# Other places for the four quarters of the input's load, for its statistics and for products of ones, in an S4D and token-mixing layer

## The chip, the core and the metric

The kernel runs on one core of a Trainium2 chip. The engines of the core work side by side, each through its own instruction stream in order: TensorE (PE; its weight loads are listed as PEld), VectorE (DVE), ScalarE (ACT), GpSimd (POOL) and SyncE (SP), which here only issues DMAs. They wait for one another through semaphores. DMAs are issued from SP's queue, and a few from GpSimd, and are moved by sixteen DMA engines. The metric is the time of one execution on the device, in microseconds.

## The reference

The layer works on x, 2048 tokens of 448 channels. It has a conditioning vector, a diagonal state-space convolution along the tokens, and a two-layer perceptron across the tokens:

```python
mod = (_silu(c) @ w_mod).reshape(c.shape[0], 6, 1, -1)
sa, ca, ga, sb, cb, gb = (mod[:, 0], mod[:, 1], mod[:, 2], mod[:, 3], mod[:, 4], mod[:, 5])
h = _layernorm(x, axis=-1) * (1 + ca) + sa
x = x + ga * _A_ref(h, A_log_A_real, A_A_imag, A_C_real, A_C_imag, A_log_dt, A_D_skip)
h = _layernorm(x, axis=-1) * (1 + cb) + sb
x = x + gb * _B_ref(h, B_w1, B_b1, B_w2, B_b2)
```

`_A_ref` first makes a convolution kernel K for every channel, as a sum over 256 complex modes of `C * exp(A * dt * position)`, and then convolves by FFT:

```python
P = jnp.exp((A * dt[:, None])[:, :, None] * pos[None, None, :])
K = 2.0 * jnp.einsum("dn,dnl->dl", C, P).real
```

## The kernel before, in words

The program has two halves. The first makes K, takes the DFT of the normalized input and of K, multiplies them and transforms back; the second is the layer norm and the perceptron. Only the beginning of the first half is touched here.

**Steps.** K is made in 56 steps (`NHALF`), one for half a group of 16 channels. A step s has these parts: TensorE makes exponents (`st_exponents`) and phases (`st_phase`, two products of the table `tab` with parameter rows and two of a rounding constant with `ones`) in PSUM; ScalarE takes exponentials of the exponents (`st_exp`, tile mag) and six activations of the phases (absolute values and sines, L677 to L682); GpSimd makes m2 (`st_mag2`: a small w, then m2, L660 and L665) and the two halves of G (L684, L685); VectorE makes the four pieces of E (L686 to L690), with `between()` called in their middle; TensorE multiplies E with G into kg (`st_kgen`, L711) two steps later.

**Sets.** Exponential and sine come from different tables of ScalarE, so eight steps (`BATCH`) form a set: `window(s)` makes all eight exponentials and the first phase, and then the eight steps run with the sine table loaded. `window(0)` is a loop over e from 0 to 7; in its passes from e = 2 on it calls `st_mag2(e - 2)`, in the passes from e = 4 on `u_stats(e - 4)`, and in pass 3 four small copies of the skip weights on GpSimd.

**The input.** The tile xt holds x, 16 rows of 448 for each of 128 partitions. `x_load(r0, n, eng)` loads n of the 16 rows by four DMAs, one for each group of 32 partitions, from SP or from GpSimd. A quarter is four rows. `u_stats(r)` makes mean and variance of row r (L513 and L514); after all sixteen, in `window(8)`, ScalarE makes the reciprocal deviations, VectorE refines them (`u_scale`) and GpSimd scales a DFT table by them (`u_table`, L529), which the first products of the input's DFT (`u_rows`, L542) need. Before, the quarters are loaded like this: the first by GpSimd in `first_chain()`, between two of its splits; the second by SP as two pairs of rows, just ahead of the loop; the third and fourth by GpSimd at the ends of steps 1 and 2. Statistics of rows 0 to 3 are made in `window(0)`, those of rows 4 to 15 two at a time in `between()` of steps 2 to 7.

**Parameters.** `first_chain()` computes the parameter rows of the first 128 channels. SP loads them straight into lex (exponents) and lph (phases) for the first groups (L867), and stores them to DRAM (pars, L871) for the later ones. `more(n)` runs steps of the same chain for the next channels on VectorE.

**Modulation.** `wm_load(k, ...)` loads one of six 448 by 448 blocks of w_mod on SP (784 KB); `modulation(k, half)` multiplies it in two parts at the ends of steps: block 1 in steps 4 and 5, block 2 in steps 6 and 7.

**Order.** On TensorE, ScalarE, VectorE and GpSimd the order of the program text is the order of execution. On SP it is that too until step 8, from where a planner orders its DMAs. `late` lists what SP issues at the start of a step. `warm(n)` multiplies the constant `ones` into a part of a PSUM tile that holds nothing at the time; its result is not used.

Of the kernel before, what the change touches and what calls it, by code (L numbers as in the profile page):

```python
# [30 lines left out]
BATCH = 8  # L31
# [189 lines left out]
def tile_adaln_s4d_mixer(ctx, tc, i, out):  # L221
# [20 lines left out]
    with ExitStack() as es:  # L242
# [94 lines left out]
        def wm_slot(k):  # L337
# [3 lines left out]


        late = {
            4: lambda: wm_load(2, wm_slot(2)),
            7: lambda: wm_load(0, wm_slot(0)),
            6: lambda: [
                nc.sync.dma_start(wu, i["WU"]),
# [309 lines left out]
        def st_mag2(s):  # L657
            me = v32(mags[s][:, 0])
            w = wp.tile([P, GD], F32, tag="w", name="w")
            G.tensor_tensor(w[:, :, None], me[:, :, 31:32], me[:, :, 1:2], ALU.mult)  # L660
            if s in (3, 4, 5):
                m2 = v32(wm0.rearrange("p k d -> p (k d)")[:, -512 * (s - 2) :][:, 0:512])
            else:
                m2 = m2p[s >= 32 and s % BATCH > 2].tile([P, GD, 32], F32, tag="m2", name="m2")
            G.tensor_tensor(m2, me, w[:, :, None].to_broadcast([P, GD, 32]), ALU.mult)  # L665
            m2s[s] = m2
# [178 lines left out]
        def first_chain():  # L845
            cr, ci, a, aim = (raws[0][nm] for nm in ("A_C_real", "A_C_imag", "A_log_A_real", "A_A_imag"))
            xa, ya, s, t, u, ph, p64 = (
                qp.tile([P, N], F32, tag=nm, name=nm) for nm in ("xa", "ya", "s", "t", "u", "ph", "p64")
            )

            w = xp.tile([P, 2, D], F32, tag="yt", name="first", bufs=3)[:, 0, 0:N]

            def split(eng, src):

                hl = room.pop()
                eng.tensor_copy(hl[:, 0].bitcast(F32R), src)
                eng.tensor_tensor(hl[:, 1].bitcast(F32R), src, hl[:, 0], ALU.subtract)
                return hl

            room = wm0.rearrange("p k d -> p (k d)")[:, -12 * N :].rearrange("p (h j n) -> p h j n", h=6, j=2)  # L860
            room = [room[:, h] for h in range(6)]
            signs = room.pop()
            sr, si_ = signs[:, 0], signs[:, 1]

            def direct(hl, tile, r, g):

                nc.sync.dma_start(tile[g][r : r + 32].bitcast(F32), hl[16 * g : 16 * g + 16])  # L867

            def store(hl, *places):
                for k, v in places:  # L870
                    nc.sync.dma_start(pars[0][v, k], hl)  # L871

            S.activation(xa, cr, AF.Abs, scale=0.5)
            S.activation(ya, ci, AF.Abs, scale=0.5)
            S.activation(a, a, AF.Exp, bias=ldt0)
            S.activation(dt[:, 0:1], ldt0, AF.Exp)

            S.activation(one, one, AF.Ln)

            ts(sr, cr, 0.0, 0.5, ALU.is_ge, ALU.subtract)  # L880
            ts(si_, ci, 0.0, 0.5, ALU.is_ge, ALU.subtract)
            tt(s, xa, ya, ALU.add)
            tt(ya, ya, xa, ALU.subtract)
            ts(s, s, 2.0**-120, None, ALU.max)
            V.reciprocal(xa, s)
            ha = split(G, a)
            tt(ya, ya, xa, ALU.mult)
            ts(t, s, 2.0**-40, 2.0**80, ALU.is_lt, ALU.mult)
            stt(p64, t, 1.0, s, ALU.max, ALU.mult)
            for g in range(4):  # L890
                direct(ha, lex, 0, g)
                if g < 3:
                    direct(ha, lex, 64, g)
            par_load(1, par_names[0:2])
            x_load(0, 4, G)
            S.activation(u, ya, AF.Square)
            S.activation(u, u, AF.Ln, bias=1.0)
            S.activation(p64, p64, AF.Ln)
            S.activation(xa, ya, AF.Arctan)
            S.activation(xa, xa, AF.Copy, scale=4 * i2p, bias=-0.5)  # L900
            S.activation(dt[:, 1:4], ldt[:, 1:4], AF.Exp)
            S.activation(sc, cvec, AF.Exp, scale=-1.0)

            ts(dt4[:, 0:1], dt[:, 0:1], 1.0 / (4 * math.pi), None, ALU.mult)
            ts(ldt2[:, 0:1], ldt0, 1.5 * math.log(2.0), None, ALU.add)
            ts(ph, aim, dt4[:, 0:1], None, ALU.mult)
            ts(w, ph, MAGIC, MAGIC, ALU.add, ALU.subtract)
            stt(s, t, -80 * math.log(2.0) / 2.0**80, p64, ALU.mult, ALU.add)
            stt(s, u, 0.5, s, ALU.mult, ALU.add)
            ts(s, s, ldt2[:, 0:1], None, ALU.add)  # L910
            hs = split(V, s)
            for g in range(4):
                direct(hs, lex, 96, g)
                if g == 0:
                    direct(ha, lex, 64, 3)
            tt(ph, ph, w, ALU.subtract)
            hp = split(G, ph)
            direct(hp, lph, 0, 0)

            ts(w, ph, MAGIC7, MAGIC7, ALU.add, ALU.subtract)  # L920
            tt(p64, ph, w, ALU.subtract)

            tt(xa, xa, sr, ALU.mult)
            stt(xa, xa, 0.5, si_, ALU.add, ALU.mult)
            stt(xa, ph, 63.0, xa, ALU.mult, ALU.add)
            ts(u, xa, MAGIC, MAGIC, ALU.add, ALU.subtract)
            tt(xa, xa, u, ALU.subtract)
            store(ha, (0, 1), (1, 1))
            hl = split(G, p64)
            direct(hl, lph, 64, 0)  # L930
            hc = split(V, xa)
            direct(hc, lph, 96, 0)
            store(hs, (2, 1))
            store(hp, (0, 0))
            store(hl, (1, 0))
            store(hc, (2, 0))
# [2 lines left out]
        par_load(1, par_names[2:4])  # L939
        for g in (1, 2):  # L940
            load(g, False)
        x_load(4, 2)
        x_load(6, 2)
        wm_load(1, wm_slot(1))
        remainder()

        def chains():
# [43 lines left out]
        def window(s):  # L991
# [11 lines left out]
            for e in range(BATCH):  # L1003
                st_exp(s + e)

                if e + 1 < BATCH:
                    st_exponents(s + e + 1)
                else:
                    st_phase(s)
                mellow()  # L1010
                flush(dve)
                flush(act)
                if s == 8 and e == 0:
                    tt(mod[1], mod[1], mod[2], ALU.mult)
                if s < 32:
                    more(WPACE[s // 8][e])
                if s == 0 and e >= 4:
                    u_stats(e - 4)
                if s == 8 and e in (3, 4):
                    modulation(0, e - 3)  # L1020
                if s == 8 and e == 5:

                    G.tensor_tensor(mod[0], mod[0], mod[2], ALU.mult)
                if s and e < (2 if s <= 32 else 1):
                    st_kgen(s - (2 if s <= 32 else 1) + e)
                elif e == 5:
                    if s == 8:
                        yks[0] = y0.tile([P, 32, DC], F32, tag="yk", name="yk0")
                    st_s1(s > 16)

                for k, e0 in ((4, 1), (5, 3), (3, 6)) if s == 16 else ():
                    if e in (e0, e0 + 1):
                        modulation(k, e - e0)

                if s == 8:
                    warm(7)
                if s in (8, 16):
                    some(u_rows, rows, (2, 2, 2, 2, 2, 0, 1, 1)[e])
                elif s == 24 and e != 5:
                    some(u_cols, cols, 1)  # L1040

                if s >= 40 and e == 2:
                    piece(False, True)
                if s >= 40 and e == 4:
                    piece(pieces[0] < NP, True)
                if s == 0 and e > 1:
                    st_mag2(e - 2)
                elif s and (e < 2 or s >= 32):
                    st_mag2(s + e)
                if s == 0 and e == 3:  # L1050
                    for r in range(4):
                        dsk_copy(r)
            aside.clear()
            if s == 0:

                S.activation(one, one, AF.Sin)


# [4 lines left out]
        for s in range(tail):  # L1063
# [20 lines left out]

            def between():
                flush(dve)
                if 2 <= s < BATCH:
                    for r in range(2 * s, 2 * s + 2):
                        u_stats(r)
                if s < len(pace):  # L1090
                    more(pace[s])

# [4 lines left out]
            else:  # L1097
                if s < 32 and s % BATCH > 1:
                    st_kgen(s - 2)
                if s % BATCH < 2:  # L1100
                    warm(10)
                if (s + 1) % BATCH:
                    st_phase(s + 1)
                elif s + 1 < NHALF:
                    st_exponents(s + 1)
                if s == 7:
                    warm(10)

                if s > 32 and s % BATCH:
                    st_kgen(s - 1)  # L1110
# [3 lines left out]
                st_kgen(s - 1)  # L1114


            if s in (1, 2):
                x_load(4 + 4 * s, 4, G)
            free = s > 7 and not st_s1(s % BATCH == BATCH - 1)
            if s + 2 < 32 and (s + 2) % BATCH > 1 and s + 2 > 5:  # L1120
                st_mag2(s + 2)
# [276 lines left out]
```

## Time and profile before

| what | before |
|---|---|
| time, median of 3 runs | 698.44 us (696.92 to 700.45) |
| the profiled execution | 699.5 us, its span 697.7 us |
| TensorE busy | 646.5 us (93%) |
| VectorE busy | 424.1 us (61%) |
| ScalarE busy | 448.5 us (64%) |
| GpSimd busy | 274.7 us (39%) |
| DMA | 128.04 MB, mean 184 GB/s |

How to read it: times in the profile count from the start of the span. A row of the timeline has start, duration, engine, line of the program, operation, result and sources, and in brackets the engine's idle time ahead of it with what ended it. A row of the chain of waits has start, duration and who worked; "issue" is time in which an engine waited for nothing that the profile shows. A row of a stretch has its limits, its length, the busy time (and count) of TensorE, its weight loads, VectorE, ScalarE and GpSimd, then the granted TensorE clock as a share of the full one, the DMA engines' busy share and GB/s. A row of a DMA queue has packets, MB and the share of the sixteen engines' time.

### The profile page before, as it was taken

To read this page: it belongs to the slowest core of one execution; us is meant where nothing else is said; L and a number is where in the kernel's file an instruction comes from. 1 tells how busy PE (TensorE), PEld (TensorE's weight loads), DVE (VectorE), ACT (ScalarE), POOL (GpSimd) and SP (SyncE) were. 2 spreads that over 40 slices of the span, in tenths; PEclk is the share of its full clock that TensorE was granted. 3 is DMA by queue.
4 is the path that set the end of the run, shared out by engine and by line. 5 is a ranking of instruction groups with operands and counts; after the bars stand their busy time and mean duration, and the time that the engine had idled before them with its cause. 6 is when DMAs were issued, how large, how long until landed. Compare 5 with 4: busy or idle time off the path is not lost.

```text
span 697.7 us, 18532 instructions
## 1 busy us (share of the span) xinstructions
PE 646.5 (93%) x7314; PEld 486.1 (70%) x7314; DVE 424.1 (61%) x811; ACT 448.5 (64%) x841; POOL 274.7 (39%) x364
## 2 busy tenths in 40 slices
PE   0868999999988899999999989999999999999997
PEld 0444454455545676676789747778999999999996
DVE  7877889787575584857744368777622354444431
ACT  5787698899879899999766568877422332222220
POOL 6694669588588767777546200000000000000000
PEclk9998999999999999999999999999999999999999
DMA  7595647588785486554579899974683445555640
GB/s 183 178 194 143 214 163 241 212 234 268 213 266 165 126 170 170 145 157 120 142 235 301 257 278 244 236 177 135 174 247 108 146 132 159 159 158 165 169 129 28
DMA packets 101894, 128.04 MB, mean 184 GB/s; under 512 B 13547, under 2 KB 85231, under 8 KB 101807
## 3 DMA queue, kind: packets, MB, share of 16 engines
q1 hardware_dynamic: 100606, 123.31, 63.0%
q0 software_dynamic: 1200, 3.54, 2.4%
q8 instruction: 58, 0.95, 0.6%
q14 instruction: 30, 0.24, 0.1%
HBM read 91.46 MB, written 34.87 MB: 181 GB/s over the span
## 4 chain that ended last, share of the span: by engine, by line
PE 68%; ACT 10%; DMA 8%; DVE 6%; issue 4%; POOL 3%; SPq 1%; DVEq 0%; ACTq 0%; POOLq 0%
PE xe L621 7%; PE acc L1222 7%; PE o L1365 6%; PE o L1364 6%; PE o L1366 6%; PE acc L1223 6%; PE acc L1224 6%; PE kg L711 6%; DMA si<-in_SK_dram 3%; PE xg L621 3%; PE pu L542 2%; PE pu L574 2%; PE vv L820 2%; PE kx L804 2%; PE vv L821 2%
## 5 line engine op out<-in xcount | busy, mean ns | idle before, releaser
L206 ACT CAST whi<-w 128x896 fp32r<-128x896 f32 x64 | 59.8, 938 | 134.9 <-PE o L1365 84.6
L215 DVE TENSOR_TENSOR wlo<-w,whi 128x896 fp32r<-128x896 f32 x64 | 68.1, 1088 | 43.1 <-ACT whi L206 36.8
L684 POOL TENSOR_TENSOR G<-mag,gs 128x512 f32<-128x512 f32 x56 | 71.9, 1283 | 50.9 <-ACT gs L680 47.1
L1222 PE MATMUL acc<-h3h,whi 128*128 128x448 f32 x224 | 82.7, 369 | 0.8 <-ACT h3h L1273 0.8
L1223 PE MATMUL acc<-h3l,whi 128*128 128x448 f32 x224 | 81.5, 364 | 0.7 <-DVE h3l L1280 0.5
L1365 PE MATMUL o<-ul,whi 128*128 128x448 f32 x224 | 81.3, 363 | 0.0
L1364 PE MATMUL o<-uh,whi 128*128 128x448 f32 x224 | 81.2, 362 | 0.0
L1224 PE MATMUL acc<-h3h,wlo 128*128 128x448 f32 x224 | 80.7, 360 | 0.0
L1366 PE MATMUL o<-uh,wlo 128*128 128x448 f32 x224 | 80.6, 360 | 0.0
L711 PEld LDWEIGHTS kg<-E,G 128*32 128x32 f32 x3584 | 56.6, 114 | 32.3 <-issue 22.2
L711 PE MATMUL kg<-E,G 128*32 128x64 f32 x3584 | 66.4, 228 | 6.7 <-issue 6.1
L685 POOL TENSOR_TENSOR G<-mag,gs 128x512 f32<-128x512 f32 x56 | 71.8, 1282 | 0.0
L621 PE MATMUL xg<-tab,lph 64*128 64x512 f32 x112 | 62.3, 556 | 5.1 <-ACT gs L680 2.4
L621 PE MATMUL xe<-tab,lph 64*128 64x512 f32 x112 | 62.2, 555 | 1.1 <-ACT gs L681 0.9
L686 DVE TENSOR_TENSOR E<-m,xe 128x512 f32<-128x512 f32 x53 | 36.4, 687 | 41.3 <-ACT xe L679 24.3
L1368 DVE SCALAR_TENSOR_TENSOR y<-o,b,mod 128x448 f32<-128x448 f32 x16 | 10.9, 684 | 80.2 <-PE o L1366 80.2
L665 POOL TENSOR_TENSOR m<-mag,w 128x512 f32<-128x512 f32 x53 | 56.0, 1056 | 4.3 <-DMA u<-us_d 0.2
L1222 PEld LDWEIGHTS acc<-h3h,whi 128*128 128x128 f32 x224 | 42.0, 188 | 13.9 <-ACT h L1278 5.6
L812 DVE TENSOR_TENSOR z<-kx,u 128x448 f32<-128x448 f32 x48 | 28.4, 620 | 27.7 <-PE kx L804 27.7
L1223 PEld LDWEIGHTS acc<-h3l,whi 128*128 128x128 f32 x224 | 42.1, 188 | 3.3 <-DVE h3l L1280 0.8
L1364 PEld LDWEIGHTS o<-uh,whi 128*128 128x128 f32 x224 | 42.0, 188 | 3.4
L621 PE MATMUL xe<-tab,lex 64*128 64x512 f32 x56 | 28.9, 531 | 16.6 <-DMA lex<-wm 15.8
(233 smaller groups left out, 1512.1 us busy)
## 6 DMA issues: line engine op xcount, KB each, us to landing
w<-in_B_w_dram SPq DMA_DIRECT2D x64, 224.0 KB
w<-in_B_w_dram SPq DMA_DIRECT2D x32, 448.0 KB
u<-us_d SPq DMA_DIRECT2D x48, 224.0 KB
yu_d<-yt SPq DMA_DIRECT2D x16, 448.0 KB
yi<-yu_d SPq DMA_DIRECT2D x32, 224.0 KB
us_d<-uo SPq DMA_DIRECT2D x16, 448.0 KB
v_d<-vt SPq DMA_DIRECT2D x32, 224.0 KB
vt<-v_d SPq DMA_DIRECT2D x16, 448.0 KB
```

The lines of the kernel that those rows point to most:

```text
L206: self.nc.scalar.copy(hi, w)
L215: eng.tensor_tensor(lo, w, hi.bitcast(F32), ALU.subtract)
L621: T.matmul(out[k], lhs[r], rhs[r], start=start, stop=stop)
L684: G.tensor_tensor(Gt[:, 1], mg_, v32(sg), ALU.mult)
L685: G.tensor_tensor(Gt[:, 0], mg_, v32(cg_), ALU.mult)
L711: T.matmul(kg[32 * q : 32 * q + 32, m], Gt[:, c, d], E[:, c, d], start=h == 0 and c == 0 and m == 0, stop=h == 1 and c == 1, skip_group_ch ...
L1222: nc.tensor.matmul(acc[f], hi[:, fs], h3h[:, r], start=r == 0, stop=False)
L1223: nc.tensor.matmul(acc[f], hi[:, fs], h3l[:, r], start=False, stop=False)
L1224: nc.tensor.matmul(acc[f], lo[:, fs], h3h[:, r], start=False, stop=r == 15)
L1364: nc.tensor.matmul(o, hi[:, ks], uh[kh][:, k], start=kh == 0 and k == 0, stop=False)
L1365: nc.tensor.matmul(o, hi[:, ks], ul[kh][:, k], start=False, stop=False)
L1366: nc.tensor.matmul(o, lo[:, ks], uh[kh][:, k], start=False, stop=kh == 1 and k == 6)
```

## The change

- The first quarter is still loaded by GpSimd, but inside `window(0)`, between w and m2 of step 0.
- The second quarter is loaded by GpSimd, at the end of pass e = 4 of `window(0)`, and no longer by SP.
- The third quarter is loaded by SP behind `wm_load(1)`, ahead of the loop; the fourth by SP at the start of step 3, behind `wm_load(2)`, which moves from step 4 to step 3.
- Statistics: rows 0 to 3 as before; rows 4 and 5 at the end of `window(0)`; row 6 in step 0, row 7 in step 1, and two rows in each of steps 2 to 5.
- `warm(4)` is new in steps 2 to 7 (the products lie between `st_kgen` and `st_phase`); the `warm(10)` of step 7 becomes `warm(16)`.

```diff
         late = {
-            4: lambda: wm_load(2, wm_slot(2)),
+            3: lambda: [wm_load(2, wm_slot(2)), x_load(12, 4)],
...
             G.tensor_tensor(w[:, :, None], me[:, :, 31:32], me[:, :, 1:2], ALU.mult)
+            if s == 0:
+                x_load(0, 4, G)
...
             par_load(1, par_names[0:2])
-            x_load(0, 4, G)
...
-        x_load(4, 2)
-        x_load(6, 2)
         wm_load(1, wm_slot(1))
+        x_load(8, 4)
         remainder()
...
+                if s == 0 and e == 4:
+                    x_load(4, 4, G)
...
             if s == 0:
-
+                u_stats(4)
+                u_stats(5)
                 S.activation(one, one, AF.Sin)
...
                 flush(dve)
-                if 2 <= s < BATCH:
-                    for r in range(2 * s, 2 * s + 2):
-                        u_stats(r)
+                for r in ((6,), (7,), (8, 9), (10, 11), (12, 13), (14, 15))[s : s + 1]:
+                    for k in r:
+                        u_stats(k)
...
                 if s % BATCH < 2:
                     warm(10)
+                elif s < BATCH:
+                    warm(4)
...
                 if s == 7:
-                    warm(10)
+                    warm(16)
...
-            if s in (1, 2):
-                x_load(4 + 4 * s, 4, G)
```

## The prediction

> **What bounds the kernel now.** I read the page first (TensorE busy 93% of a 697.7 us span), then, because every edit lies in the first 70 us, the chain of waits of 26 to 75 us:
>
> ```profile
> 48.93 4.23 issue
> 53.16 0.43 PE kg L711 x6
> 53.60 0.72 PE xe L621
> ...
> 56.43 1.79 PE pm L498 x2
> ...
> 61.27 0.04 ACT ab L677
> ...
> 70.39 0.41 POOL wur L529
> ```
>
> The chain runs from engine to engine, so in this stage no engine alone sets the time. Its longest piece is no arithmetic: TensorE stands still for 4.23 us. What the chain feeds is the sine set: from 61.27, when ScalarE starts the last sines (step 7), a fixed sequence leads to the first scaled DFT table at 70.39. So **the moment the sines of step 7 can start is my measure**: what moves it moves all behind it.
>
> The timeline of VectorE says what holds step 7 back. It makes the E products (L686 to L690) of steps 0 to 7 and the statistics (L513) between them:
>
> ```profile
> 21.81 0.62 DVE L513 BATCH_NORM_STATS2 st<-xt 128x6 f32<-128x448 f32 x1
> ...
> 27.69 0.18 DVE L514 BATCH_NORM_AGGREGATE mv<-st 128x2 f32<-128x6 f32 x1
> 30.60 0.69 DVE L686 TENSOR_TENSOR E<-m,xe 128x512 f32<-128x512 f32 x1 [2.73 <-ACT xe L679]
> 31.21 0.68 DVE L687 SCALAR_TENSOR_TENSOR E<-mag,xe 128x512 f32<-128x512 f32 x1
> ...
> 32.55 1.38 DVE L415 SCALAR_TENSOR_TENSOR s<-t,s 128x256 f32<-128x256 f32 x1
> ...
> 51.52 0.63 DVE L513 BATCH_NORM_STATS2 st<-xt 128x6 f32<-128x448 f32 x1 [4.62 <-DMA xt<-in_A_u_dram]
> ...
> 52.28 0.59 DVE L513 BATCH_NORM_STATS2 st<-xt 128x6 f32<-128x448 f32 x1
> ...
> 57.43 0.68 DVE L690 TENSOR_TENSOR E<-wm,xg 128x512 f32<-128x512 f32 x1
> ```
>
> One row's statistics cost 0.76 us (52.28 minus 51.52), a piece of E 0.6 (31.21 minus 30.60), and two operations of the parameter chain in step 0 some 2.1 (31.8 to 33.9). VectorE idles 2.73 us before step 0 and 4.62 us in step 4, there for the third quarter of the input. GpSimd issues that quarter in step 1, and its own timeline shows the prices of issuing:
>
> ```profile
> 8.74 2.29 POOL L300 DMA_DIRECT2D xt<-in_A_u_dram  x4
> ...
> 15.27 0.78 POOL L857 TENSOR_TENSOR wm<-p,wm 128x256 fp32r<-128x256 f32 x1
> 17.27 0.27 POOL L660 TENSOR_TENSOR w<-mag 128x16 f32<-128x16 f32 x1 [1.23 <-ACT mag L644]
> 17.62 1.19 POOL L665 TENSOR_TENSOR m<-mag,w 128x512 f32<-128x512 f32 x1
> 21.23 0.30 POOL L660 TENSOR_TENSOR w<-mag 128x16 f32<-128x16 f32 x1 [2.42 <-ACT mag L644]
> ...
> 22.75 1.33 POOL L482 COPY dsk<-dskr 1x112 f32<-1x112 f32 x4
> ...
> 31.09 1.27 POOL L684 TENSOR_TENSOR G<-mag,gs 128x512 f32<-128x512 f32 x1 [1.42 <-ACT gs L680]
> ...
> 37.60 2.20 POOL L300 DMA_DIRECT2D xt<-in_A_u_dram  x4
> ...
> 42.26 2.20 POOL L300 DMA_DIRECT2D xt<-in_A_u_dram  x4
> ```
>
> How long such a quarter takes to arrive is in the view of the input tile, for these three groups of four DMAs (from issue to landing, shortest, median, longest):
>
> ```profile
> DMA to landing us min/median/max: 5.7/6.4/7.3
> DMA to landing us min/median/max: 8.5/10.3/12.1
> DMA to landing us min/median/max: 10.5/11.6/12.4
> ```
>
> Four issues take 2.2 to 2.3 us, so the last one starts 1.7 us after the first, and a quarter is complete 9.0 us after its first issue in the first case (17.7) and 13.8 us after it in the second (51.4, where VectorE's wait ends).
>
> **The change part by part.**
>
> *First quarter, moved into set 0.* GpSimd is free at 16.05 (15.27 + 0.78); w of step 0 takes 0.3, then the four issues 2.2, ending at 18.6, then m2 1.2. Before, GpSimd waited 2.42 us for step 1's magnitudes at that place, so the issues cost GpSimd nothing. If that wait shrank, up to 2.2 us would move onto m2 of step 1, which VectorE needs only after step 0. The DMA side gains and loses. It gains because the rows of the exponents, which SP loads in the same time, come sooner:
>
> ```profile
> 17.22 3.22 SPq L867 DMA_DIRECT2D lex<-wm  x5
> ...
> 30.03 6.09 SPq L300 DMA_DIRECT2D xt<-in_A_u_dram  x8
> ```
> ```profile
> 19.24 0.79 PE L621 MATMUL xg<-tab,lex 64*128 64x512 f32 x1 [2.68 <-DMA lex<-wm]
> ```
>
> TensorE's wait for them, 2.68 us, is the most that set 0 can start earlier. It loses because the quarter's first issue is now at 16.4 and it is complete at 25.4 (9.0) to 30.2 (13.8), while VectorE asks for it at 21.81. From that first row's statistics to the end of the fourth's VectorE needs 6.1 us (21.81 to 27.87), so it is done at 31.5 to 36.3 at the earliest. The earlier start of set 0 is thus worth nothing: VectorE, not ScalarE, comes last before step 0.
>
> *Second quarter, from SP to GpSimd, behind m2 of step 2.* GpSimd: 18.6 + 1.2 (m2 of step 0) = 19.8; w and m2 of step 1 to 21.3; the four copies 1.3; step 2's pair 1.4, so the first issue is at 24.1 and the last at 25.8. The three pairs behind it (1.3 each) end at 30.2, before G of step 0 would start (31.09): hidden. Its statistics of rows 4 and 5 stand ahead of step 0's products. Complete: at 31.5 if the last DMA takes the shortest landing shown (25.8 + 5.7), 33.1 with 9.0, 37.9 with 13.8. I take 33.1, the first row, since there too GpSimd's queue held this one quarter, while in the second case the fourth was queued right behind it. Step 0 then starts at 33.1 + 2 x 0.76 = **34.6 instead of 30.60: +4.0 us**; bounds 33.0 (+2.4) and 39.4 (+8.8).
>
> *Third and fourth quarters, from GpSimd to SP.* GpSimd loses 2 x 2.20 us of issuing among the G products; SP loses eight issues (6.09 us with their waits) and gains eight of larger size. The modulation weights 1 now come before the third quarter and weights 2 before the fourth; both are wanted later (steps 4 and 6) and only gain. Behind the fourth quarter on SP stand the exponent rows of set 8, due at the end of step 7. The third quarter is wanted in step 2: 34.6 + 5.2 (step 0: four pieces of E, one row, the parameter chain) + 3.2 (step 1: four pieces, one row) + 1.2 (two pieces) = 44.2. SP's issues for it start near 30 to 31 (where 30.03 was); 13.8 us after 30.4 is 44.2. So by the worse row it is just in time, by the better 4.8 us early. **The wait of 4.62 us goes: -4.6.** Bounds: all of it, or about 2 left.
>
> *Statistics in other steps.* Sixteen rows as before. Between the start of step 0 and the end of step 5 there are ten of them (6 to 15) instead of eight (4 to 11): +2 x 0.76 = **+1.5**. Steps 6 and 7 have none; they lay beside ScalarE's sines and saved nothing on the path.
>
> *From the end of step 5 to the sines of step 7.* Before, step 5 ended at 58.11 (57.43 + 0.68), the sines began at 61.27: 3.16 us, because TensorE was late and slow:
>
> ```profile
> 18.00:22.00 4.00, 2.50 (x7) 1.36 (x7) 3.76 (x13) 1.93 (x5) 1.50 (x3) 1.00 0.21 48
> ...
> 53.50:60.00 6.50, 6.46 (x77) 3.43 (x74) 6.40 (x15) 3.93 (x8) 2.77 (x3) 0.51 0.30 74
> 60.00:64.00 4.00, 4.00 (x93) 2.49 (x90) 2.98 (x7) 2.73 (x6) 1.51 (x3) 1.00 0.43 105
> ```
> ```profile
> 60.00 0.50 PE L621 MATMUL xe<-tab,lph 64*128 64x512 f32 x1
> ...
> 63.32 1.27 PE L633 MATMUL kg<-ones 128*128 128x256 bf16 x10
> ...
> 70.84 0.98 PE L542 MATMUL pu<-xt,wur 32*64 32x449 f32 x8 [1.51 <-POOL wur L529]
> ```
>
> The granted clock (third number from the end) is 0.51 after the standstill, 1.00 from 60 on. At full clock a step's phase takes 1.3 us (60.00 to 61.27), and it needs only step 5's buffers. Without the standstill TensorE is on time: 1.3 instead of 3.2, **-1.9**; bounds -1.9 and 0.
>
> *More products of ones.* 0.127 us each at full clock (1.27 for ten). Four more in each of steps 2 to 7 are 0.5 us a step beside VectorE's 3.9 (four pieces, two rows); six more in step 7 are 0.8 us and fall into TensorE's 1.51 us wait before 70.84: nothing. If that cover went, they would cost 0.5 and 0.8.
>
> *A cold clock after the new wait.* TensorE now has nothing between the phase of step 1 and the end of step 0's products. A cold phase took 2.8 us (53.60 to 56.43) against 1.3, so the second phase can be late by 0 to 1.6; I take the middle, **+0.8**, since VectorE is busy with step 1 for a part of it.
>
> **Sum**: +4.0 - 4.6 + 1.5 - 1.9 + 0.8 = -0.2 us. The profiled execution took 699.5 us (span 697.7 and 1.8 around it), 1.1 over the median of 698.44, and would take 699.3; the median gives 698.2. Bounds of all terms: with 33.0, no cold phase and the chain's 1.38 us operation at some 0.4 (what others on 128x256 take in VectorE's timeline), -3.6, so 694.8; with 39.4 and a full cold phase, +5.4, so 703.8.
>
> **The rivals.**
>
> 1. *The second quarter comes late and step 0 waits: slower.* The last part of the sum hangs on who gets the DMA engines. Two stretches of the DMA view, GpSimd's queue being q0 and SP's q1:
>
> ```profile
> q0 software_dynamic: 152, 0.54, 85.3%
> q1 hardware_dynamic: 83, 0.08, 15.4%
> q8 instruction: 1, 0.02, 2.8%
> ```
> ```profile
> q1 hardware_dynamic: 191, 0.34, 91.4%
> q0 software_dynamic: 12, 0.04, 12.0%
> ```
>
> From 50 to 53 us GpSimd's queue had 85% of them, from 46 to 48 SP's had 91%, with an input quarter still open. [...] Worked from rows: while the second quarter moves (26 to 34 us) SP has the stores of four parameter tables, modulation weights and the third quarter. If they get what they got from 46 to 48, it is complete 13.8 us after its issue, at 37.9, step 0 starts at 39.4, and the sum is +4.6: **703.0**. It decides from a landing after 33.3, where the sum is zero. For it: two of three groups took that long. Against: the first did not. Chance 0.25.
>
> 2. *Everything lands quickly: faster.* With the shortest landing (31.5), no cold phase and the chain's operation at 0.4: **694.8**, a little less if the phases run ahead. For it: the DMA engines were busy for only 0.21 of their time from 18 to 22 us (the first of the three stretches above). Against: the first quarter and the rows and stores that come sooner fill just that hole. Chance 0.15.
>
> 3. *It does not remove the standstill.* The 4.23 us of TensorE are labelled "issue", and an instruction packet (q8, the row above) was moved between 50 and 53: TensorE lacked instructions while the input filled the DMA engines. If that happens again, or the third quarter is late, some 2 us of the -4.6 return: **700.2**. Chance 0.10.
>
> **How the numbers follow.** The forecast, 698.2 with its own range of 695.5 to 701, has 0.50. A measurement of this kernel tells about 0.5% (3.5 us) from no change: faster is below 694.95, slower above 701.93. Forecast and rival 3 lie within; rival 1 lies above with nine tenths of its chance, rival 2 around the lower bound, with a little from the forecast's edge: faster 0.15, same 0.61, slower 0.24. Range 693.8 to 703.5: it takes in both rivals' times.
>
> **What would show it.** Right: VectorE waits for the input before step 0's statistics of rows 0 and 4 and no longer in step 4; step 0's first E product at 33 to 36; set 0's second exponent product near 17; the sines of step 7 near 61; the granted clock 1.00 from 53 to 60. Wrong: E of step 0 before 32 (the quarters land faster than any shown) or after 38 (rival 1); a TensorE standstill in steps 3 to 6; a difference that arises behind 71 us, where I have put none, though SP's order is planned anew there.

## The result, and the profile after

| | before | after |
|---|---|---|
| time, median of 4 runs each | 697.68 us (696.53 to 700.45) | 708.17 us (706.28 to 709.65) |
| ratio, with its 95% interval | | 1.0113 (1.0069 to 1.0157) |
| the profiled execution (its span) | 699.5 us (697.7) | 708.6 us (706.8) |
| sines of step 7 start | 61.27 us | 62.82 us |
| first DFT product starts | 70.84 us | 73.69 us |
| mean granted clock of the profiled execution | 0.988 | 0.981 |

The change made the kernel 1.1% slower by the ratio; the two medians of four differ by 1.5%, which lies within its interval. The prediction was 698.2 us within 693.8 to 703.5: wrong, outside the range and past its own slower rival (703.0). Line numbers from L679 on are two higher than before. Six executions of the experiments ran in a slower state, and the ratios and clocks are without them (three of the twelve of e2, its profiled one among them, and one each of e3, e6 and e10).

The timeline of VectorE after, where the prediction had its terms (start, duration, operation, and in brackets the idle time ahead with what ended it):

```profile
23.89 0.61 DVE L513 BATCH_NORM_STATS2 st<-xt 128x6 f32<-128x448 f32 x1
...
33.48 0.63 DVE L513 BATCH_NORM_STATS2 st<-xt 128x6 f32<-128x448 f32 x1 [3.88 <-DMA xt<-in_A_u_dram]
...
34.96 0.67 DVE L688 TENSOR_TENSOR E<-m,xe 128x512 f32<-128x512 f32 x1
...
37.20 0.42 DVE L415 SCALAR_TENSOR_TENSOR s<-t,s 128x256 f32<-128x256 f32 x1
...
42.95 0.68 DVE L689 SCALAR_TENSOR_TENSOR E<-mag,xe 128x512 f32<-128x512 f32 x1
46.28 0.63 DVE L513 BATCH_NORM_STATS2 st<-xt 128x6 f32<-128x448 f32 x1 [2.65 <-DMA xt<-in_A_u_dram]
...
55.11 0.63 DVE L513 BATCH_NORM_STATS2 st<-xt 128x6 f32<-128x448 f32 x1 [1.06 <-DMA xt<-in_A_u_dram]
...
61.02 0.68 DVE L692 TENSOR_TENSOR E<-wm,xg 128x512 f32<-128x512 f32 x1
```

One wait of 4.62 us has become three, of 3.88, 2.65 and 1.06. The first is the predicted one, ahead of step 0. The second stands in step 2: VectorE had done its first two pieces of E at 43.6 (42.95 + 0.68), and the third quarter was there only at 46.2. The chain of waits after (start, duration, who worked) runs through that quarter and not through the second one:

```profile
25.68 7.86 DMA lph<-pars
...
33.56 12.64 DMA xt<-in_A_u_dram
...
46.28 0.64 DVE st L513
...
65.68 1.87 PE kg L633 x16
...
67.57 0.37 ACT ks L727
```

It also shows why the quarter is late. SP issues its last DMA only at 33.56, once the load of lph issued at 25.68 has landed, and this DMA takes 12.64 us. SP's queue in the timeline after, and SP's longest wait from 29 to 35 us (in total, times, longest):

```profile
28.90 0.43 SPq L325 DMA_DIRECT2D wm<-in_w_mod_dram  x1
29.37 4.50 SPq L300 DMA_DIRECT2D xt<-in_A_u_dram  x4
```
```profile
SPq L300 <- DMA lph<-pars: 2.6, 1, 2.6
```

Four issues that took GpSimd 2.2 us take SP 4.50, and 2.6 of these are that wait. The last two lines of that chain are the second new thing: ScalarE's copy of kg, which stands ahead of the logarithms and of the two table loads (1.28 us each) that lead to the DFT table, waits for the products of ones, which are written into the same tile. The two timelines of ScalarE at that copy, before and then after:

```profile
64.70 0.40 ACT L725 COPY ks<-kg 128x256 f32<-128x256 f32 x1
```
```profile
67.57 0.37 ACT L727 COPY ks<-kg 128x256 f32<-128x256 f32 x1 [1.20 <-PE kg L633]
```

The lead of before is thus 1.55 us at the sines of step 7 and 2.85 at the first DFT product. Behind that it grows, and the granted clock (third number from the end of a row) shows where. Stretches of after, then the same stretches of before:

```profile
34.50:45.00 10.50, 6.84 (x84) 4.00 (x84) 8.58 (x18) 3.17 (x7) 3.83 (x4) 0.51 1.07 203
53.50:60.00 6.50, 5.38 (x95) 2.75 (x92) 5.34 (x12) 4.85 (x11) 6.31 (x8) 1.00 0.21 61
75.40:78.80 3.40, 3.40 (x65) 2.19 (x58) 2.26 (x5) 1.20 (x3) 2.95 (x6) 0.51 0.48 174
150.50:153.90 3.40, 3.40 (x32) 1.40 (x34) 2.77 (x5) 3.37 (x8) 3.32 (x4) 0.51 0.81 185
224.00:250.00 26.00, 20.85 (x382) 13.66 (x383) 11.07 (x18) 22.01 (x42) 19.16 (x26) 0.80 0.57 142
```
```profile
34.50:45.00 10.50, 8.06 (x215) 5.64 (x215) 9.95 (x21) 9.64 (x20) 9.85 (x13) 0.90 0.83 190
75.40:78.80 3.40, 3.40 (x30) 1.41 (x29) 3.33 (x7) 2.15 (x5) 2.65 (x5) 1.00 0.76 277
150.50:153.90 3.40, 3.40 (x76) 1.92 (x75) 3.40 (x7) 3.39 (x8) 3.32 (x5) 1.00 0.79 237
224.00:250.00 26.00, 23.59 (x446) 15.77 (x436) 14.37 (x26) 23.07 (x46) 18.79 (x22) 0.93 0.63 133
```

The half clock of 53 to 60 us is gone, as predicted (1.00). Other stretches of it have come instead: in the first wait, right behind the first DFT product and at 150 (0.51 each), and around 235 (0.80 over 224 to 250, against 0.93). Behind 100 us TensorE has the same products to make in both kernels, and at 150 it takes longer for them. The products of yi, before and then after:

```profile
145.84 1.74 PE L574 MATMUL pu<-yi,s 128*128 128x448 f32 x4
```
```profile
150.23 3.02 PE L574 MATMUL pu<-yi,s 128*128 128x448 f32 x4
```

Ahead of them TensorE idles 0.22 and 1.05 us in both kernels, and only after has the half clock. They start 4.4 us later than before, and what follows them on ScalarE 6.0. The span ends 9.1 later. So of the loss 1.5 us lie ahead of the sines of step 7, 1.3 between them and the first DFT product, 1.5 more by 80 us, and 4.7 behind that.

### The profile page after: what moved, and what is told of

It reads as the page before. It is cut to its first block, busy times and chain, and to the rows that moved or that the text cites. A ratio compares the mean times of both kernels' runs of the same rounds, so it can differ in the third digit from the quotient of the medians.

```text
span 706.8 us, 18584 instructions
## 1 busy us (share of the span) xinstructions
PE 651.7 (92%) x7344; PEld 488.2 (69%) x7344; DVE 424.2 (60%) x811; ACT 448.4 (63%) x841; POOL 272.8 (39%) x360
## 4 chain that ended last, share of the span: by engine, by line
PE 73%; ACT 8%; DMA 7%; DVE 7%; issue 3%; POOL 1%; SPq 1%; DVEq 0%; ACTq 0%; POOLq 0%
PE xe L621 7%; PE acc L1225 6%; PE o L1368 6%; PE o L1367 6%; PE o L1369 6%; PE acc L1226 6%; PE acc L1227 6%; PE kg L713 6%; PE vv L822 3%; PE kx L806 3%; PE vv L823 3%; PE pu L542 3%; PE pu L574 3%; PE xg L621 2%; PE kg L633 2%
## 5 line engine op out<-in xcount | busy, mean ns | idle before, releaser
L679 ACT ACTIVATE ab<-xe 128x512 f32<-128x512 f32 x56 | 33.9, 605 | 22.5 <-PE xg L621 11.2
```

## The experiments

Fourteen kernels ran, in four groups; each group has its own runs of before (medians 698.13, 699.94, 699.44 and 699.22 us), so kernels are compared by their ratios to these. The clock is the mean of the granted clock over the executions that the ratio counts; the two milestones, in us, come from the one profiled execution of each kernel, so they vary with its clock (none is given for e2).

| kernel | ratio (95% interval) | clock | sines of step 7 | first DFT product |
|---|---|---|---|---|
| before | 1 | 0.987 | 61.27 | 70.84 |
| after | 1.0113 (1.0069, 1.0157) | 0.982 | 62.82 | 73.69 |
| e1 | 1.0103 (1.0071, 1.0134) | 0.977 | 62.88 | 72.58 |
| e2 | 1.0061 (1.0031, 1.0090) | 0.987 | | |
| e3 | 1.0123 (1.0081, 1.0166) | 0.981 | 62.26 | 72.47 |
| e4 | 1.0112 (1.0079, 1.0145) | 0.981 | 63.14 | 73.82 |
| e5 | 0.9976 (0.9948, 1.0005) | 0.988 | 54.81 | 65.47 |
| e6 | 1.0012 (0.9979, 1.0045) | 0.989 | 54.11 | 66.36 |
| e7 | 1.0160 (1.0125, 1.0195) | 0.982 | 62.86 | 73.73 |
| e8 | 1.0045 (1.0019, 1.0071) | 0.986 | 60.80 | 70.49 |
| e9 | 1.0021 (1.0002, 1.0040) | 0.985 | 59.21 | 69.43 |
| e10 | 1.0068 (1.0034, 1.0101) | 0.981 | 62.44 | 72.07 |
| e11 | 0.9967 (0.9945, 0.9990) | 0.989 | 54.40 | 66.32 |
| e12 | 1.0024 (0.9996, 1.0053) | 0.983 | 55.32 | 66.93 |
| e13 | 1.0047 (1.0022, 1.0071) | 0.983 | 60.13 | 70.40 |
| e14 | 1.0064 (1.0038, 1.0090) | 0.984 | 59.30 | 70.57 |

**The products of ones: e1 takes the added ones out of the changed kernel, e2 adds them to the kernel before (the same edits the other way), e3 keeps the added four a step in steps 2 to 7 and takes back the six of step 7 (the second edit alone).**

```diff
                 if s % BATCH < 2:
                     warm(10)
-                elif s < BATCH:
-                    warm(4)
...
                 if s == 7:
-                    warm(16)
+                    warm(10)
```

> The changed kernel without its additional products of ones (no warm(4), warm(10) again in step 7); loads and statistics as changed. Theory A (the loss has two roots: the input's third and fourth quarter wait on SP, worth 1.6 us at the sines of step 7, and the longer run of ones in step 7, worth 1.3 us because ScalarE's copy of kg waits for it): the sines of step 7 stay near 62.8 us, the copy behind them comes 1.3 us sooner, the first scaled DFT product at 72 to 72.5 instead of 73.7; time 1.5 to 5 us below the changed kernel, 703 to 707. Theory B (the loads alone make the loss, products of ones are free): within 1 us of the changed kernel, 707 to 709.

> The kernel before with only the additional products of ones. Theory A: the copy of kg behind the sines of step 7 comes 0.8 to 1.3 us later than before, the time is 1 to 3 us above before (699 to 701); if the 60 further TensorE instructions also move the places where TensorE lacks instructions, a standstill labelled issue appears at another place than 48.9 us. Theory B: within 0.5 us of before.

> The changed kernel with ten products of ones in step 7 as before, the four in steps 2 to 7 kept. Theory A: sines of step 7 unchanged near 62.8, the copy of kg behind them near 66.8 instead of 67.6, first scaled DFT product near 72.9 to 73.0, time 0.8 to 2 us below the changed kernel. Theory B: no difference.

From the sines of step 7 to the first DFT product it takes 9.57 us before, 9.70 in e1 (copy of kg at 66.46, no wait), 10.21 in e3 and 10.87 after. So the copy does wait for the added ones, and they cost this stretch 1.2 us. The whole time hardly follows: e1 is as slow as after within the intervals, e3 too, as theory B had it. In e1 the clock is lower (0.977), and already its first DFT product is slow (1.77 us against 0.98). Added to the kernel before, the ones cost 0.6%, more than either theory had; no profile of a counted execution shows where. So they are a loss there, while in the changed kernel taking them out brings only 0.1%, with intervals that overlap: what they cost depends on the kernel around them, and they don't explain this loss.

**The third and fourth quarters: e4 puts them ahead of the modulation weights on SP.**

```diff
-        wm_load(1, wm_slot(1))
         x_load(8, 4)
+        wm_load(1, wm_slot(1))
...
-            3: lambda: [wm_load(2, wm_slot(2)), x_load(12, 4)],
+            3: lambda: [x_load(12, 4), wm_load(2, wm_slot(2))],
```

> The changed kernel with the third quarter ahead of modulation weights 1 and the fourth ahead of weights 2 on SP. Theory A (the quarters wait behind the weights): the third quarter's wait of 2.65 us in step 2 falls below 0.5, the fourth's of 1.06 in step 4 goes, the sines of step 7 come at 60 to 61.5 instead of 62.8, time 1 to 3 us below the changed kernel unless the weights now come late for step 4. Rival (the DMA engines are full whatever the order): waits within 1 us of the changed kernel's and the same time.

The four issues now take SP 2.34 us, and VectorE no longer waits for the third quarter. SP's wait has not gone: it now stands ahead of the weights' issue behind them, 2.1 us from 31.96 (29.62 + 2.34) to 34.06.

```profile
29.62 2.34 SPq L300 DMA_DIRECT2D xt<-in_A_u_dram  x4
34.06 0.31 SPq L325 DMA_DIRECT2D wm<-in_w_mod_dram  x1
```

So the 2.6 us in after hang on the quarter's place in SP's order, behind an unfinished load; that the weights' 784 KB hold it up is not shown. But VectorE's wait for the fourth grew from 1.06 to 2.02 us, and TensorE stands still for 2.08 us at 54.6 with no releaser in the profile and then runs at half clock (0.51 from 56.7 to 60.1). The sines of step 7 start at 63.14, no earlier. The expected gain was given back before it reached them; this run doesn't tell what the third quarter's wait is worth.

**The places of the statistics: e5 has the input's new order, the old places of the statistics and no added ones (both edits of e1 come to those shown); e6 has the added ones too.**

```diff
-                u_stats(4)
-                u_stats(5)
...
-                for r in ((6,), (7,), (8, 9), (10, 11), (12, 13), (14, 15))[s : s + 1]:
-                    for k in r:
-                        u_stats(k)
+                if 2 <= s < BATCH:
+                    for r in range(2 * s, 2 * s + 2):
+                        u_stats(r)
```

> The input in the new order, the statistics of the rows where the kernel before has them, no added products of ones. Theory A (the changed kernel loses by where its statistics stand and by the added products, not by the order of the loads): step 0 waits for no quarter, its first E product starts near 30.6 us as in the kernel before; the third quarter is there at about 46.3, so step 4 waits 0 to 2 us in place of 4.62; the sines of step 7 start at 58.5 to 60.5 (61.27 before, 62.82 after); TensorE idles at most 2 us ahead of the first DFT product, no half clock between 68 and 80; 694 to 698.5 us. Rival B (the order of the loads costs it, whatever the statistics do): sines of step 7 at 62 or later, first DFT product at 72.5 or later, 703 to 708 us.

> The kernel of e5_old_places_of_statistics with the added products of ones of the changed kernel. Theory A: the copy of kg to ks in step 7 waits for the 16 products, so the stretch from the sines of step 7 to the first DFT product grows from about 9.6 to 10.2-10.9 us; 1 to 4 us longer than e5. Rival (the ones keep the clock up and pay for themselves): mean granted clock 0.002 or more above e5's and a time equal or lower.

This is the run that decides. VectorE's timeline in e5, with step 0's first E and the first row of the third quarter:

```profile
29.83 0.67 DVE L688 TENSOR_TENSOR E<-m,xe 128x512 f32<-128x512 f32 x1
...
47.12 0.62 DVE L513 BATCH_NORM_STATS2 st<-xt 128x6 f32<-128x448 f32 x1
```

VectorE waits for the input nowhere: the quarter that comes at 46 is asked for at 47.12. The sines of step 7 start at 54.81, 6.5 us ahead of the kernel before and 8.0 ahead of the changed one, and the ratio falls from 1.0103 (e1, the same kernel with the new places) to 0.9976. The order of the loads is thus no loss; theory A holds, B falls. The milestone came earlier than A expected (58.5 to 60.5), since the clock stayed full from 34.5 to 45 us too (1.00, against 0.90 before). That is in part luck of the profiled execution: its mean clock is 0.995, that of all twelve 0.988. But e11 and e12 below, whose profiled executions are close to their medians, reach the sines at 54.40 and 55.32. In e6 the copy of kg waits 2.57 us for the ones, and the first DFT product is 0.9 us later than in e5; the ratio rises by 0.36%, with intervals that overlap.

**The hole ahead of the DFT table: e7 fills it in the changed kernel with ones (first diff), e8 makes one in the kernel before by taking the statistics out of steps 6 and 7 (second).**

```diff
                 if s == 8:
-                    warm(7)
+                    warm(7 if e else 24)
```
```diff
-                if 2 <= s < BATCH:
-                    for r in range(2 * s, 2 * s + 2):
+                if 2 <= s < 6:
+                    for r in range(2 * s, 2 * s + 2) if s < 5 else range(10, 16):
```

> The changed kernel with 24 products of ones in place of 7 in the stretch in which TensorE waits 3.07 us for the table of the first DFT product; nothing waits for them before that table is ready. Theory A (that idle time brings the half clock at 75): no half clock between 70 and 80, products of 75 us back from 1.61 to 1.1 us, mean granted clock 0.983 to 0.986, 704.5 to 707 us. Rival (half clock has another cause or more ones cost as much as they bring): half clock still there or time 708 to 710 us.

> The kernel before with the statistics of rows 12 to 15 moved from steps 6 and 7 into step 5 and nothing else. Theory A (statistics in the last steps keep TensorE's last work of the set late and so its idle time short): E of step 7 ends about 1 us earlier at about 65.8, TensorE idles 2.3 to 3.2 us ahead of the first DFT product in place of 1.51, a half clock follows between 68 and 80; 699 to 701 us. Rival (the place of the last statistics does not matter): idle 1.5 to 1.9 us, no half clock there, 697 to 699 us.

TensorE's timeline in e7:

```profile
69.73 2.79 PE L633 MATMUL kg<-ones 128*128 128x256 bf16 x24
73.73 0.98 PE L542 MATMUL pu<-xt,wur 32*64 32x449 f32 x8 [1.21 <-POOL wur L529]
...
75.08 1.10 PE L713 MATMUL kg<-E,G 128*32 128x64 f32 x64
...
89.16 1.98 PE L751 MATMUL y<-wc,ks 64*64 64x64 f32 x62 [2.15 <-DVE yt L545]
```

The products at 75 are back at 1.10 us (1.61 after), but TensorE falls idle again at 87, now for VectorE, and is slow from there (1.98 us, the clock 0.52 from 88 to 95, where after has 1.00). The time is no better. Filling that hole only moved the half clock, so theory A falls here as to the time. In e8 TensorE's timeline has the hole without the lateness:

```profile
70.49 0.98 PE L542 MATMUL pu<-xt,wur 32*64 32x449 f32 x8 [2.73 <-POOL wur L529]
...
72.05 1.93 PE L711 MATMUL kg<-E,G 128*32 128x64 f32 x64
```

The sines of step 7 and the first DFT product come 0.5 and 0.35 us earlier than before, the products behind them take 1.93 us in place of 1.10 (the clock is 0.63 from 70.5 to 74.5, 1.00 before), and the ratio is 1.0045. That agrees with theory A, at a price of some 3 us (0.45% of 699; 1.3 to 5 by the interval). That the half clock is what costs them is not shown: the mean clock is 0.986 against 0.987, and the span of the profiled execution is only 1.2 us longer.

**The waits one by one: e9 has only that for the second quarter, e10 only that for the third, e13 brings the third quarter's back by a single row, e14 takes it out of the changed kernel.** Each is e5 or after with other rows in the lookup by step, which in after is `((6,), (7,), (8, 9), (10, 11), (12, 13), (14, 15))`:

```
 e9:  rows 4, 5 at the end of set 0; {3: (6, 7), 4: (8, 9), 5: (10, 11), 6: (12, 13), 7: (14, 15)}
 e10: {1: (4, 5), 2: (6, 7, 8, 9), 3: (10, 11), 4: (12, 13), 5: (14, 15)}
 e13: {2: (4, 5, 8), 3: (6, 7), 4: (9,), 5: (10, 11), 6: (12, 13), 7: (14, 15)}
 e14: rows 4, 5 at the end of set 0; {0: (6,), 1: (7,), 4: (8, 9), 5: (10, 11), 6: (12, 13), 7: (14, 15)}; ones as after
```

> The kernel of e5_old_places_of_statistics with rows 4 and 5 at the end of set 0, as in the changed kernel; rows 6 to 15 stay in steps 3 to 7. Only the wait for the second quarter is left. Both theories: first E product of step 0 at 34.5 to 35.3 us, no wait for the third or fourth quarter. Theory C (of the three waits of the changed kernel the third quarter's sets the end, the second's is hidden behind it): sines of step 7 at 56.5 to 58.5 us, 698 to 702 us. Rival D (the second quarter's wait, the one the prediction priced, is the whole loss): sines of step 7 at 61 or later, 705 to 709 us.

> The kernel of e5_old_places_of_statistics with the statistics early except for rows 4 and 5: rows 4 and 5 in step 1, 6 to 9 in step 2, 10 and 11 in step 3, 12 and 13 in step 4, 14 and 15 in step 5. Step 0 waits for nothing, step 2 waits for the third quarter. Theory C: first E product of step 0 near 30, a wait of 4 to 6.5 us in step 2 that ends at 46.0 to 46.6 like the changed kernel's, sines of step 7 at 61 to 63 us, 704 to 708 us. Rival D: sines of step 7 at 57 to 59 us, 698 to 702 us.

> The kernel of e5_old_places_of_statistics with one statistic moved: row 8, the first of the third quarter, from step 4 into step 2 (row 9 stays in step 4). VectorE then waits in step 2 until the quarter is there at 46 to 47 us, but steps 6 and 7 keep their statistics. Theory G (the late start of all that follows is the loss): sines of step 7 at 61.5 to 63.5 us, 704 to 708 us. Rival H (part of the loss is that steps 6 and 7 have no statistics and TensorE falls idle early): sines as late, TensorE idles under 2 us ahead of the first DFT product, 700 to 703.5 us.

> The changed kernel with the statistics of rows 8 to 15 put back into steps 4 to 7; rows 4 to 7 stay early, the added products of ones stay. Theory C (the third quarter's wait sets the end): the wait for the second quarter stays, step 0's first E product at about 35; no wait of over 0.6 us for the third or fourth; sines of step 7 at 58 to 60.5 us; 700 to 704.5 us. Rival D (the second quarter's wait and the ones are the loss): sines at 61.5 or later, 706 to 709 us.

VectorE's wait in e9, then in e10, then in e13:

```profile
34.36 0.63 DVE L513 BATCH_NORM_STATS2 st<-xt 128x6 f32<-128x448 f32 x1 [4.21 <-DMA xt<-in_A_u_dram]
```
```profile
46.74 0.63 DVE L513 BATCH_NORM_STATS2 st<-xt 128x6 f32<-128x448 f32 x1 [5.97 <-DMA xt<-in_A_u_dram]
```
```profile
45.78 0.63 DVE L513 BATCH_NORM_STATS2 st<-xt 128x6 f32<-128x448 f32 x1 [4.86 <-DMA xt<-in_A_u_dram]
```

With the second quarter's wait alone the sines start at 59.21, 4.4 us later than in e5 and later than theory C expected. With the third quarter's alone they start at 62.44, as late as after: step 2 can't go on before 46 to 47 us, whether step 0 waited or not. So at the milestone the third quarter's wait sets the end, and the second's is hidden behind it but for 0.4 us (theory C). In e13 one row of sixteen in the earlier step costs 0.71% against e5, some 5 us. Its sines came at 60.13, earlier than both theories expected; its ratio, 1.0047 against 1.0068 for e10, points the way of theory H, but the intervals overlap. In e14 the changed kernel keeps its other edits and gets rows 8 to 15 back into steps 4 to 7: the sines start at 59.30, as theory C expected, and the ratio falls from 1.0113 to 1.0064.

**What could be better: e11 puts rows 4 and 5 into VectorE's idle time in step 1 of e5, e12 also leaves only 2 ones in step 7.** The rows by step are `{1: (4, 5), 2: (6, 7), 4: (8, 9), 5: (10, 11), 6: (12, 13), 7: (14, 15)}` in both; e12 has this too:

```diff
                 if s == 7:
-                    warm(10)
+                    warm(2)
```

> The kernel of e5_old_places_of_statistics with rows 4 and 5 in step 1 and 6 and 7 in step 2, none in step 3; 8 to 15 stay. VectorE is idle 1.47 us between steps 1 and 2 there and hardly from 38 to 61. Theory E (VectorE sets the pace of steps 2 to 7): sines of step 7 1.0 to 1.5 us earlier, at 53.3 to 53.8; median 0.5 to 2 us below e5's. Rival F (the matrices of step 2 are late for ScalarE whatever VectorE does, or the third quarter at 46.3 is too late for step 4): sines at 54.5 or later, no gain.

> The kernel of e11_statistics_in_the_gap with 2 products of ones in step 7 in place of 10. Theory A (ScalarE's copy of kg waits for them): that copy 0.9 to 1.0 us earlier against the sines of step 7, first DFT product 0.9 us earlier, TensorE idle ahead of it under 1.7 us; 0.5 to 1.5 us below e11. Rival (the ones hold the clock): a half clock between 55 and 75 us and a time equal to or above e11's.

e11 is the fastest kernel here: 0.33% under before, an interval that just leaves 1 out, which is weak evidence for the best of fourteen. Its sines are only 0.4 us ahead of e5's and the two can't be told apart, so theory E's gain isn't shown. e12 refutes theory A where the ones were too few. A stretch of e12 and a row of its TensorE timeline:

```profile
60.00:64.00 4.00, 3.42 (x32) 1.26 (x34) 2.47 (x6) 3.96 (x8) 0.01 (x1) 0.50 0.63 171
```
```profile
63.31 1.93 PE L713 MATMUL kg<-E,G 128*32 128x64 f32 x64
```

TensorE ran at half clock there (0.50), the products of kg took 1.93 us, and e12 is 0.6% slower than e11. TensorE is slow there in e11 too (two products of pm take 1.70 us at 59.96, 1.02 at 76.22), but the same products of kg, at 62.31, take only 1.27. The mean clock over all executions is 0.983 in e12 and 0.989 in e11: here fewer ones went with a lower clock and a longer time, though the copy waits 1.06 us for them in e12 and 2.24 in e11.

## Why the prediction was wrong, by its own steps

**Right.** Step 0's first E product at 34.6: it was 34.96, the wait being the second quarter's, complete at 33.4 where 33.1 was taken. (In this two errors of about half a us cancel: its first issue came at 23.64 and not 24.1, and it took 9.7 us and not 9.0.) The two more rows of statistics are +1.5 as said. TensorE's standstill and the half clock of 53 to 60 us went, and from the end of step 5 (61.70) to the sines it is 1.12 us where 1.3 was said. The clock was 0.51 after the new wait, as said, though it cost VectorE nothing: it idled 0.41 us ahead of step 2 as before, where +0.8 had been taken. One sign was wrong without harm: VectorE did not wait for the first quarter, which was there 7.1 us after its first issue and not 9.0 to 13.8.

**The step that failed first** is that of the third quarter: "just in time", "The wait of 4.62 us goes: -4.6", with 2 us left at worst. VectorE asked for it at 43.6 (44.2 was said), but it came at 46.2, 16.8 us after SP's first issue, not 13.8. The duration had been taken from GpSimd, whose last issue starts 1.7 us after the first; on SP it started 4.2 after it, because of the wait for lph, and that is most of the difference. With the fourth quarter's 1.06, waits of 3.71 us stayed where nothing was to be left: the term is -0.9. That the sum at the milestone is nevertheless only 1.55 us and not 3.5 comes from that cold phase and from the parameter chain's two operations in step 0, some 2.1 us before and 0.6 after, which the prediction had only among its bounds.

**The step that put the time outside the range** is another one: "what moves it moves all behind it", with nothing put behind 71 us. Even with -0.9 for that term the sum would have been +3.5, or 701.9 us, inside the range, and the milestone came only 1.55 us late. Of the 9.1 us by which the span grew, 7.5 arise behind the milestone, 1.3 up to the first DFT product and 6.2 (9.1 less 2.85) behind it, where after has more of the half clock (0.51 for 1.00 at 75.4 and at 150.5, 0.80 for 0.93 over 224 to 250). The other kernels say the same, as far as single profiles can: e9, e13 and e14 reach the sines 1.1 to 2.1 us earlier than before and are 0.21% to 0.64% slower, and e5 reaches them 6.5 us earlier for 0.24%. Part of the reason shows: in e6, e11 and e12, which come to the sines earliest with e5, the stretch from there to the first DFT product grows from 9.57 us to between 11.6 and 12.2; in e12 TensorE waits in it for the exponent rows of set 8 (0.51 and 0.90 us).

**The upper bound was too low by its own terms.** 703.8 left out two bounds that stand in the text, "about 2 left" of the third quarter's wait and 0 for the standstill. With them it is +9.3, or 707.7. That this is close to the measured 708.17 would have been luck, since most of the loss lies elsewhere.

**Rival 1 named the wrong quarter.** It said that a late second quarter would decide. It came as forecast, and its wait alone costs 3.1 us (e9 against e5); the third quarter's alone costs 6.4 us (e10 against e5). At the milestone of the changed kernel the second's is hidden behind the third's. In the time it may not be: e1, which has both waits, is 0.35% above e10, with intervals that overlap.

**"Nothing" for the ones** was wrong for the sixteen of step 7. They were laid beside TensorE's wait ahead of the first DFT product, but the wait they lengthen is ScalarE's, for the tile they write. The price said in case that cover went, 0.8 us, is near the 0.66 by which e3 shortens the stretch.

**Statistics in steps 6 and 7 "saved nothing on the path".** Right for the milestone, wrong for the time: taking them out made the kernel before 0.45% slower (e8).

**The half clock.** In after the stretches at 75.4 and 150.5 have a clock of 0.51 for 3.4 us each, where before has 1.00. The idle time ahead did not tell where it comes: ahead of the second it is the same in both kernels (0.22 and 1.05 us), and an idle time ahead of the first DFT product of 1.62 us has the half clock behind it in e9 (0.50 from 70.6 to 74), one of 2.68 does not in e6 (1.00 from 66 to 72). What sets it, no run here shows. The mean clock also differs between executions of one kernel, from 0.979 to 0.995 for before. What chance hardly explains is that kernels differ in the mean over all their executions, 0.987 for before and 0.982 for after.

**What stays open** is that last point, and with it the path of most of the 6.2 us. The kernels whose step 2 waits for the third quarter (after, e1, e3, e7, e10, e13), and e4, which waits 2.0 us for the fourth, have mean clocks of 0.977 to 0.983; the others have 0.983 to 0.989. In the profiled execution of after a part of this lies behind 100 us, where every kernel does the same work: 0.80 in the stretch of 224 to 250, 0.93 before. Why, no run here shows.

So the loss is that of the statistics' places, 1.3% between e1 and e5, which differ in nothing else, and the new order of the loads would not have needed it. How it comes about is shown up to the first DFT product, and only seen behind it. That order alone is 0.24% faster than before, or no different (0.9948 to 1.0005).

## What to carry to other kernels

A consumer moved ahead of the moment its data can be there turns slack into a wait, also for what stands behind it (in e10 5.97 us on VectorE, and sines of step 7 that start 7.6 us later than in e5): look up when the load really lands, on the queue that will issue it, before putting its reader earlier. When a transfer changes queues, take its duration from that queue, with what stands ahead of it (the third quarter took 16.8 us on SP, not 13.8). A point in the middle of a program tells what happens up to it; that the end moves by as much has to be looked up too (1.55 us at the sines, 9.1 at the end). And products that nobody reads are not free when another engine waits for the tile they write (ScalarE's copy of kg waited 1.20 us for them).

## What the runs showed of the hardware

- Over 238 executions of these kernels and of before, compared within each kernel and group, 0.001 less of mean granted clock goes with 0.51 us more (standard error 0.03). The 0.0057 between after and before go with 2.9 us by that, about a third of the loss.
- The same four DMAs of 224 KB keep SP for 4.50 us in after and for 2.34 us in e4, and four such keep GpSimd for 2.29 and 2.21 us in after. In SP's 4.50 lie waits of 2.9 us for earlier loads to land (2.6 for lph, 0.3 for A_A_imag): an issue that looks long can be a wait for another transfer.
- TensorE idled 0.22 and 1.05 us ahead of the products of yi both before and after, with the same instructions between, and only after ran them at half clock (3.02 us against 1.74).
- More products of ones did not raise the mean clock: 0.982 in e7 with its 24 in the hole, 0.987 in e2, against 0.982 and 0.987 without. Fewer went with a lower one in e1 (0.977) and e12 (0.983, with 0.989 in e11), but not in e5 (0.988, as in e6).
